# A PSUM bank for the weight conversion's intermediate, taken from the attention's products with v

## The chip, the cores and the metric

The kernel runs on one core of one Trainium2 chip. The metric is the device time of one launch in microseconds (us), lower is better. The core has TensorE (PE in the profile) for matmuls, VectorE (DVE), ScalarE (ACT) and GpSimd (POOL) for elementwise work, and SyncE (SP), which here only issues transfers. The engines run their own instruction rows in order and wait for one another through semaphores. Tiles live in SBUF or in PSUM; PSUM has eight banks of 2 KB a partition, and one bank holds 512 float32 values a partition.

## The reference

Sixteen attention heads (2 batches of 8, 768 tokens, head size 64) attend only inside hash buckets, and two gated MLPs follow (1536 tokens, model size 512, hidden size 2048):

```python
q_bits = (np.einsum('bhsd,dk->bhsk', q, proj) > 0); k_bits = (np.einsum('bhsd,dk->bhsk', k, proj) > 0)
mask = q_bucket[:, :, :, None] == k_bucket[:, :, None, :]        # the six bits read as a number
scores = np.where(mask, scale * np.matmul(q, k.transpose(0, 1, 3, 2)), -1e9)
x = softmax(scores) @ v                                           # heads side by side: 1536 x 512
h = x @ w_in;  g = h * (1.0 / (1.0 + np.exp(-1.702 * h)));  x = g @ w_out
h = x @ w_in2; g = h * (1.0 / (1.0 + np.exp(-h)));          out = g @ w_out2
```

The four weight matrices arrive as 64-bit floats. The kernel turns them into 32-bit ones itself.

## The kernel before, in words

**Stages.** The first batch's attention runs first, alone (to about 145 us of the span). Then the second batch's attention runs with the first MLP of the first batch's tokens laid between its steps (to about 415 us): this is the stretch that the change touches, and it is called the mixed stretch below. After it come the rest of that MLP, the first MLP of the second batch's tokens, and the second MLP.

**Attention.** A step is one head and one block of 128 query tokens. `scores` (L414, L415) puts a step's 128x768 scores into a `pss` tile of two banks; DVE's `top` (L422) takes them out to `p` and finds the extreme of each row, ACT takes the exponential (L427) and a half-precision copy `hl` (L438), POOL the remainder of that copy (L442), and a transposing transfer brings both as `pt` (L448). `av` (L460 to L462) multiplies `pt` with the head's v, three matmuls for each of six blocks of keys, into `pav`. All the steps of a head (half of them for the last two heads of a batch) go to one `pav` bank and make a group. `norm` (L472 to L476) divides the group's products by their sums on DVE. After every second head `x_turn` (L488) transposes the result through a `psx` bank and `x_split` (ACT L494, DVE L495) takes it out of there. In the mixed stretch there is one `pss` tile, so a step's scores wait until the DVE has taken the last step's.

**MLP.** `gemm1` (L624) makes twelve matmuls into a `psh` bank for a block of 384 tokens and 128 hidden units. ACT (L629) and DVE (L630) gate it, ACT and POOL split it (L634, L635). `gemm2` (L658) multiplies with the second weight matrix, and DVE adds the result to `part` (L667). Every product is made of three matmuls of a high and a low part.

**Weights.** A chunk is 128x512 weights. `Weights.step` fetches a chunk to `raw` (L139) and converts it: ACT takes the absolute value of the upper words (L170), four DVE operations of 128x512 elements follow, clamp (L171), shift (L172), and two that merge in words of `raw` (L173, L175), each rewriting the SBUF tile `f`; then ACT writes the high part (L177) and POOL the low part (L178). `f` has two buffers. There are 64 chunks, 28 of which the change touches; of the others four come before the point of the program at which the mixed stretch begins, and 32 belong to the second MLP.

**Who sets the order.** The program lists its work step by step; a scheduler then sorts each engine's instructions, with priorities by kind of task (the table SOONER, left as it is). `RATE` sets how many MLP pieces go with one attention step, and a chunk is converted with each piece while there is room for it.

**PSUM.** In the mixed stretch the banks are: two for `m` (`pstr`, the transposes of q and k, and `psbit`), two for `av` (`pav` and `psx` in turn), two for `pss`, two for `psh` and `pso`.

Of the kernel before, what the change touches and what calls it, by code (L numbers as in the profile page):

```python
# [9 lines left out]
F32 = mybir.dt.float32  # L10
F32R = mybir.dt.float32r
F16 = mybir.dt.float16
I32 = mybir.dt.int32
I64 = mybir.dt.int64
AF = mybir.ActivationFunctionType
ALU = mybir.AluOpType
AX = mybir.AxisListType
PSUM = bass.MemoryType.PSUM
# [3 lines left out]
def tile_lsh_attention_two_mlps(  # L22
# [13 lines left out]
    V, A, G, T, SP = nc.vector, nc.scalar, nc.gpsimd, nc.tensor, nc.sync  # L36
# [5 lines left out]
    P = 128  # L42
# [5 lines left out]
    NDC = DM // P  # L48
# [9 lines left out]
    TINY = 2.0 ** -15  # L58
    HUGE = 122880.0 - 2.0 ** -7
# [47 lines left out]
    class Weights:  # L107
# [41 lines left out]
        def step(self):  # L149
            n = self.done  # L150
            depth = 3 if late[0] is not None else 1
            while self.issued <= min(n + depth, len(self.chunks) - 1):
                self.fetch()
            i, kind = self.chunks[n]
            pool = self.pool_of(i)[0]
            hi = pool.tile([P, NDC, P], F32R, tag=f"w{kind}h", name=f"w{kind}h")
            lo = pool.tile([P, NDC, P], F32R, tag=f"w{kind}l", name=f"w{kind}l")
            block = self.order[i]
            self.t[i, kind] = hi, lo
            self.done += 1  # L160
            if self.again(n):
                for t, d in zip((hi, lo), self.kept.pop((block, kind))):
                    SP.dma_start(out=t.bitcast(F32), in_=d)
                return
            raw = self.raw.pop(n)
            word = raw.bitcast(I32).rearrange("p c (e w) -> p c e w", w=2)
            f = (late[0] or wpool).tile([P, NDC, P], F32, tag="f", name="f", bufs=2 if late[0] else FB)
            fi = f.bitcast(I32)
            top, bot = word[:, :, :, 1], word[:, :, :, 0]
            A.activation(f, top.bitcast(F32), AF.Abs)  # L170
            V.tensor_scalar(f, f, TINY, HUGE, op0=ALU.max, op1=ALU.min)  # L171
            V.tensor_scalar(fi, fi, 3, 0x3FFFFFFF, op0=ALU.logical_shift_left, op1=ALU.bitwise_and)  # L172
            V.scalar_tensor_tensor(out=fi, in0=top, scalar=-0x40000000, in1=fi,  # L173
                                   op0=ALU.bitwise_and, op1=ALU.bitwise_or)
            V.scalar_tensor_tensor(out=fi, in0=bot, scalar=29, in1=fi,  # L175
                                   op0=ALU.logical_shift_right, op1=ALU.bitwise_or)
            A.copy(hi, f)  # L177
            G.tensor_tensor(out=lo, in0=f, in1=hi.bitcast(F32), op=ALU.subtract)  # L178
            if self.last[block] > i:
                self.kept[block, kind] = []  # L180
                for t, part in ((hi, "h"), (lo, "l")):
                    d = spill.tile([P, NDC, P], F32, name=f"sp{kind}{part}{block[1]}")
                    SP.dma_start(out=d, in_=t.bitcast(F32))
                    self.kept[block, kind].append(d)
# [64 lines left out]
    def attention(sp, s1, ps_m, ps_v, ahead_of, setup):  # L249
        nat, st = {}, {}  # L250
# [4 lines left out]
        for n in range(0, HEADS, 2):  # L255
            parts = 2 if n % H == H - 2 else 1
            for half in range(parts):
                for h in (n, n + 1):
                    w = NC // parts
                    g = tuple(range(len(steps), len(steps) + w))  # L260
# [4 lines left out]
        count = {"nv": 0}  # L265
# [94 lines left out]

        def rows_at_once(half):
            for nm, i, w in (("k", 0, thr), ("q", 2, thrq)):
                ps = ps_v.tile([P, 512], F32, tag="av", name="psbit")
                o, cols = ps[0:R, 0:HS], slice(i * R, (i + 1) * R)
                T.matmul(o, lhsT=pa[i][:, cols], rhs=st[nm, 0][:, half], start=True, stop=False)
                T.matmul(o, lhsT=pb[i][:, cols], rhs=st[nm, 0][:, half], start=False, stop=True)
                dst = (BQ if nm == "q" else BK)[0]
                V.tensor_scalar(dst[0:R, half * HS:(half + 1) * HS], o, w[0:R, 0:1], w[0:R, 1:2],
                                op0=ALU.is_ge, op1=ALU.mult)
# [81 lines left out]
        def av(j):  # L451
            (n, c), g = steps[j], group[j]
            vs, s = st["v", n // 2]
            pt = st.pop(("pt", j))
            if j == g[0]:
                st["av", g] = ps_v.tile([P, 512], F32, tag="av", name="pav")
            o = st["av", g][:, c * (D + 1):(c + 1) * (D + 1)]
            for i in range(NC):
                hv, lv = vs[:, n % 2, i, 0:D + 1], vs[:, n % 2, i, D + 1:]
                T.matmul(o, lhsT=pt[:, i], rhs=hv, start=(i == 0), stop=False)  # L460
                T.matmul(o[:, 0:D], lhsT=pt[:, i], rhs=lv, start=False, stop=False)
                T.matmul(o, lhsT=pt[:, NC + i], rhs=hv, start=False, stop=(i == NC - 1))  # L462
# [20 lines left out]
                    x_split(pr, half)  # L483

        def x_turn(pr, half):
            ps = ps_v.tile([P, 512], F32, tag="av", name="psx")
            for d in range(HC):
                T.transpose(ps[:, d * P:(d + 1) * P], st["x", pr][:, half * HC + d].rearrange("p j d -> p (j d)"), ident)  # L488
            st["px", pr, half] = ps[:, 0:HS]
# [6 lines left out]


        asked = set()

        def ahead(pr, s):  # L500
            a, b = 2 * pr, 2 * pr + 1
# [34 lines left out]
        for n in (0, 1):  # L536
# [15 lines left out]
            for half in range(2):  # L552
                if n == 0:
                    rows_at_once(half)
                else:
                    bits(0, half, (1, 3))
                    signs(0, half)
# [17 lines left out]
        for lead, first, last in ((2, 0, N // 2), (1, N // 2, N)):  # L575
# [5 lines left out]
            for i in range(first - lead, last + LAG + 1):  # L581
# [4 lines left out]
                m = i - LAG  # L586
# [3 lines left out]
                m = i - 2 * (2 - lead)  # L590
# [98 lines left out]
    again = [NF - 1 - RING - i for i in range(NF - RING)]  # L689
    order = [(0, f) for f in range(NF)] + [(0, f) for f in again] + [(1, f) for f in range(NF)]  # L690
    late = [None]

    def pool_of(i):
        if i < NF:
            return wpool, i - RING if i >= RING else None
        slot = (i - NF) % (RING + RING2)
        before = i - RING - RING2
        if slot < RING2:
            return late[0], before if before >= NF else None
        return wpool, before if before >= NF else NF - RING + slot - RING2  # L700
# [6 lines left out]
    def background():  # L707
        if W.can_step():
            with sooner("weights"):
                W.step()  # L710

    with ExitStack() as es:
        ps_m = es.enter_context(tc.tile_pool(name="ps_m", bufs=2, space=PSUM))
        ps_v = es.enter_context(tc.tile_pool(name="ps_v", bufs=2, space=PSUM))
        sp = es.enter_context(tc.tile_pool(name="att", bufs=2))
        s1 = es.enter_context(tc.tile_pool(name="att1", bufs=1))
        ps_s = ExitStack()
        am = ps_s.enter_context(tc.tile_pool(name="att2", bufs=1))
        ahead_of = {"lead": 2, "more": {t: (am, MORE[t]) for t in MORE if MORE[t]}}
        ahead_of["pool"] = ps_s.enter_context(tc.tile_pool(name="ps_s", bufs=2, space=PSUM))  # L720
        gen, credit = None, 0.0
        for i in attention(sp, s1, ps_m, ps_v, ahead_of, lambda: attention_setup(sp, s1, am, ps_m)):
            if i == -2:
                for _ in range(EARLY):
                    W.fetch()
            if gen is None and i >= WSTART and i % WEVERY == 0 and W.done < 4:
                W.step()
            if gen is None and i == SWITCH - 1:
                ps_s.close()
                stage[0] = 1  # L730
                ahead_of["lead"] = 1
                ahead_of["more"] = {}
                mb = es.enter_context(tc.tile_pool(name="mlpb", bufs=2))
                ahead_of["pool"] = es.enter_context(tc.tile_pool(name="ps_s1", bufs=1, space=PSUM))
                ps_h = es.enter_context(tc.tile_pool(name="ps_h", bufs=2, space=PSUM))
                gen = mlp(0, [0, 1], [[f, f + 1] for f in range(0, NF, 2)], W, mb, ps_h, True, first1)
            if gen is not None:
                credit += RATE[i >= 3 * HEADS // 4 * NC]
                while credit >= 1.0:
                    credit -= 1.0  # L740
                    next(gen, None)
                    background()
        for _ in gen:
            background()
    stage[0] = 2
    late[0] = ctx.enter_context(tc.tile_pool(name="w2", bufs=RING2))
    mp = ctx.enter_context(tc.tile_pool(name="mlp", bufs=2))
    ps_h = ctx.enter_context(tc.tile_pool(name="ps_h", bufs=8, space=PSUM))
# [35 lines left out]
```

## Time and profile before

| what | value |
|---|---|
| time, median of 3 runs | 829.68 us (829.2 to 832.83) |
| the profiled execution: its time, its span | 829.76 us, 827.9 us |
| granted TensorE clock, mean | 0.965 |
| PE busy: whole span; 0 to 145, 145 to 415, 415 to 828 us | 748.4; 108.87, 235.72, 403.78 us |
| DVE busy in the same stretches | 539.1; 117.04, 229.18, 192.89 us |
| ACT busy | 421.9; 99.25, 174.63, 147.97 us |
| POOL busy | 443.2; 94.13, 189.60, 159.47 us |

The profiled execution lies 0.08 us above the median, and its span leaves 1.9 us around it. The stretches are read with one row of a table that gives each engine's busy time in each window. "Busy" covers an instruction from its start to its end, so time in which it is held up after its start counts as busy too.

### The profile page before, as it was taken

The page shows a single profiled execution, that of the slowest core. Times are in us where ns is not written, and L with a number is a line of the kernel's source. Part 1 is how long each engine was busy: PE and PEld are TensorE (multiplying, and loading weights), DVE is VectorE, ACT ScalarE, POOL GpSimd, SP SyncE. Part 2 cuts the span into 40 slices and gives each one's busy share as a digit, 9 for nine tenths or more (in the row PEclk, how much of TensorE's full clock was granted, in tenths as well). Part 3 has the DMA queues.
Part 4 walks back from the last instruction along what each step waited for, and adds up shares of the span by engine and source line. Part 5 has one row for each costly group of instructions (what it writes and reads, how often), then busy time and mean ns, then how long its engine had stood idle before and what let it go on. Part 6 is the DMA issues. An engine that isn't in the chain of part 4 may idle for free.

```text
span 827.9 us, 14002 instructions
## 1 busy us (share of the span) xinstructions
PE 748.4 (90%) x5384; PEld 687.0 (83%) x5384; DVE 539.1 (65%) x932; ACT 421.9 (51%) x721; POOL 443.2 (54%) x345
## 2 busy tenths in 40 slices
PE   6786787688888989898999999979999999999998
PEld 5675666678787878787999999978999889988996
DVE  8886788889799988888524243899733843422222
ACT  5776567585766757566544232444545423321220
POOL 5675576777766767566733242648534533421120
PEclk9898998799999999999999999999999999999999
DMA  5999999999989878874688431233310300000112
GB/s 155 198 198 187 185 215 199 239 251 252 252 211 243 221 210 204 204 168 79 115 285 287 141 114 40 84 120 101 103 51 28 126 1 1 0 1 1 39 39 76
DMA packets 196270, 116.40 MB, mean 141 GB/s; under 512 B 153318, under 2 KB 175846, under 8 KB 196204
## 3 DMA queue, kind: packets, MB, share of 16 engines
q1 hardware_dynamic: 196044, 115.52, 55.3%
q8 instruction: 42, 0.69, 0.3%
q14 instruction: 24, 0.20, 0.1%
q10 hardware_dynamic: 160, 0.00, 0.0%
HBM read 56.63 MB, written 16.78 MB: 89 GB/s over the span
## 4 chain that ended last, share of the span: by engine, by line
PE 59%; DVE 20%; DMA 8%; issue 6%; ACT 5%; POOL 2%; SPq 0%; DVEq 0%; ACTq 0%; POOLq 0%
PE pso L658 26%; PE psh L624 25%; DMA pt<-hl 5%; DVE f L173 3%; DVE p L422 3%; DVE f L171 3%; DVE f L175 2%; DVE f L172 2%; DMA raw<-in_moe_w_in_dram 2%; PE pss L414 2%; DVE part L667 1%; ACT p L427 1%; PE psbit L342 1%; PE pss L415 1%; PE pav L460 1%
## 5 line engine op out<-in xcount | busy, mean ns | idle before, releaser
L635 POOL TENSOR_TENSOR gl<-g,gh 128x384 fp32r<-128x384 f32 x128 | 138.3, 1082 | 195.1 <-ACT gh L634 182.3
L442 POOL TENSOR_TENSOR hl<-p,hl 128x768 f16<-128x768 f32 x96 | 168.0, 1757 | 83.3 <-ACT hl L438 38.3
L624 PE MATMUL psh<-XH,wih 128*128 128x384 f32 x512 | 174.7, 341 | 2.9 <-DVE part L667 2.9
L624 PE MATMUL psh<-XL,wih 128*128 128x384 f32 x512 | 173.6, 339 | 2.2 <-DVE XL L495 2.2
L624 PE MATMUL psh<-XH,wil 128*128 128x384 f32 x512 | 173.7, 339 | 0.0
L633 DVE TENSOR_TENSOR g<-g,psh 128x384 f32<-128x384 f32 x96 | 52.8, 551 | 117.3 <-ACT g L632 117.3
L667 DVE SCALAR_TENSOR_TENSOR part<-pso,part 128x384 f32<-128x384 f32 (+1 forms) x124 | 72.5, 590 | 83.6 <-PE pso L658 83.4
L427 ACT ACTIVATE p<-p,lo 128x768 f32<-128x768 f32 x96 | 89.6, 937 | 69.8 <-DVE p L422 69.6
L634 ACT CAST gh<-g 128x384 fp32r<-128x384 f32 x128 | 65.5, 512 | 84.0 <-DVE g L633 70.2
L658 PE MATMUL pso<-gh,woh 128*128 128x384 f32 x256 | 89.0, 354 | 15.2 <-DVE g L630 5.5
L624 PEld LDWEIGHTS psh<-XH,wih 128*128 128x128 f32 x512 | 97.6, 191 | 4.4 <-DVE part L667 2.6
L624 PEld LDWEIGHTS psh<-XL,wih 128*128 128x128 f32 x512 | 97.5, 190 | 3.1 <-DVE XL L495 2.5
L422 DVE TENSOR_SCALAR_CACHE_REDUCE p<-pss 128x768 f32<-128x768 f32 x96 | 90.4, 946 | 12.1 <-PE pss L415 9.9
L624 PEld LDWEIGHTS psh<-XH,wil 128*128 128x128 f32 x512 | 97.6, 191 | 0.2 <-POOL wil L178 0.2
L632 ACT ACTIVATE g<-psh 128x384 f32<-128x384 f32 x96 | 46.8, 489 | 97.0 <-PE psh L624 96.0
L414 PE MATMUL pss<-ak,aq 128*128 128x384 f32 x192 | 76.4, 399 | 18.1 <-DVE p L422 17.8
L460 PE MATMUL pav<-VS,pt 128*128 128x65 f16 x576 | 65.1, 200 | 25.8 <-DMA pt<-hl 24.5
L658 PE MATMUL pso<-gh,wol 128*128 128x384 f32 x256 | 86.5, 338 | 0.0
L658 PE MATMUL pso<-gl,woh 128*128 128x384 f32 x256 | 86.5, 338 | 0.0
L460 PEld LDWEIGHTS <-pt 128*128 128x128 f16 x576 | 54.7, 100 | 33.7 <-DMA pt<-hl 28.5
L658 PE MATMUL pso<-woh,gh 128*128 128x512 f32 x192 | 74.8, 390 | 0.3 <-ACT gh L634 0.3
L658 PE MATMUL pso<-wol,gh 128*128 128x512 f32 x192 | 75.0, 391 | 0.0
(114 smaller groups left out, 1616.9 us busy)
## 6 DMA issues: line engine op xcount, KB each, us to landing
raw<-in_moe_w_in_dram SPq DMA_DIRECT2D x32, 512.0 KB
raw<-in_moe_w_out_dram SPq DMA_DIRECT2D x32, 512.0 KB
spih<-wih SPq DMA_DIRECT2D x13, 256.0 KB
spil<-wil SPq DMA_DIRECT2D x13, 256.0 KB
spoh<-woh SPq DMA_DIRECT2D x13, 256.0 KB
spol<-wol SPq DMA_DIRECT2D x13, 256.0 KB
wih<-spih SPq DMA_DIRECT2D x13, 256.0 KB
wil<-spil SPq DMA_DIRECT2D x13, 256.0 KB
```

The source lines that it names most:

```text
L414: T.matmul(o, lhsT=lq, rhs=ak[:, half, :], start=True, stop=False)
L422: V.tensor_scalar(p, st.pop(("S", j)), LOW, None, op0=ALU.min, op1=ALU.min, accum_out=lo)
L427: A.activation(p, p, AF.Exp, bias=lo, scale=-1.0)
L442: G.tensor_tensor(out=hl[:, 1], in0=st.pop(("p", j))[0], in1=hl[:, 0], op=ALU.subtract)
L460: T.matmul(o, lhsT=pt[:, i], rhs=hv, start=(i == 0), stop=False)
L624: T.matmul(h, lhsT=a[:, c], rhs=x[t][:, c], start=(n == 0), stop=(n == 3 * NDC - 1))
L632: A.activation(g, h, AF.Sigmoid, scale=beta)
L633: V.tensor_tensor(out=g, in0=g, in1=h, op=ALU.mult)
L634: A.copy(gh[:, f], g)
L635: G.tensor_tensor(out=gl[:, f], in0=g, in1=gh[:, f].bitcast(F32), op=ALU.subtract)
L658: T.matmul(y, lhsT=a, rhs=x, start=(n == 0), stop=(n == 3 * nf - 1))
L667: V.scalar_tensor_tensor(out=acc, in0=y, scalar=scale, in1=acc, op0=ALU.mult, op1=ALU.add)
```

## The change

The tile `f` is split in two roles. A new tile `u` takes the absolute value and the three in-place operations; the fourth one reads `u` and writes `f`, which ACT and POOL then read from SBUF as before. In the mixed stretch `u` is a PSUM tile of one bank with one buffer; everywhere else `u` is `f` itself, and the instructions are what they were.

The bank comes from `av`. Its pool of two buffers becomes two pools of one, used in turn by `v_bank`. At the start of the mixed stretch the second is closed: `pav` then has one bank, and `x_turn` takes its `psx` from the two `m` banks.

```diff
+            u = work[0].tile([P, NDC, P], F32, tag="u", name="u") if work[0] is not None else f
+            ui = u.bitcast(I32)
-            A.activation(f, top.bitcast(F32), AF.Abs)
-            V.tensor_scalar(f, f, TINY, HUGE, op0=ALU.max, op1=ALU.min)
-            V.tensor_scalar(fi, fi, 3, 0x3FFFFFFF, op0=ALU.logical_shift_left, op1=ALU.bitwise_and)
-            V.scalar_tensor_tensor(out=fi, in0=top, scalar=-0x40000000, in1=fi,
+            A.activation(u, top.bitcast(F32), AF.Abs)
+            V.tensor_scalar(u, u, TINY, HUGE, op0=ALU.max, op1=ALU.min)
+            V.tensor_scalar(ui, ui, 3, 0x3FFFFFFF, op0=ALU.logical_shift_left, op1=ALU.bitwise_and)
+            V.scalar_tensor_tensor(out=ui, in0=top, scalar=-0x40000000, in1=ui,
                                    op0=ALU.bitwise_and, op1=ALU.bitwise_or)
-            V.scalar_tensor_tensor(out=fi, in0=bot, scalar=29, in1=fi,
+            V.scalar_tensor_tensor(out=fi, in0=bot, scalar=29, in1=ui,
                                    op0=ALU.logical_shift_right, op1=ALU.bitwise_or)
...
-                ps = ps_v.tile([P, 512], F32, tag="av", name="psbit")
+                ps = v_bank("psbit")
...
-                st["av", g] = ps_v.tile([P, 512], F32, tag="av", name="pav")
+                st["av", g] = v_bank("pav")
...
-            ps = ps_v.tile([P, 512], F32, tag="av", name="psx")
+            ps = v_bank("psx") if len(ps_v) > 1 else ps_m.tile([P, 512], F32, tag="m", name="psx")
...
+        def v_bank(name):
+            j = count["av"] = (count.get("av", -1) + 1) % len(ps_v)
+            return ps_v[j].tile([P, 512], F32, tag="av", name=name)
...
-        ps_v = es.enter_context(tc.tile_pool(name="ps_v", bufs=2, space=PSUM))
+        ps_v = [es.enter_context(tc.tile_pool(name="ps_v", bufs=1, space=PSUM))]
...
+        ps_v.append(ps_s.enter_context(tc.tile_pool(name="ps_x", bufs=1, space=PSUM)))
...
                 ps_s.close()
+                ps_v.pop()
...
+                work[0] = es.enter_context(tc.tile_pool(name="ps_w", bufs=1, space=PSUM))
...
     stage[0] = 2
+    work[0] = None
```

The scheduler sorts the rows anew. Row texts carry each program's own line numbers: L170 to L173, L175 and L177 of before are L173 to L176, L178 and L180 of the changed kernel, L422 is L425, L427 is L430, L438 is L441, and L629, L630 and L634 are L637, L638 and L642.

First, DVE's row early in the mixed stretch, before: conversions (`f`), scores taken out (`p`) and gates (`g`).

```order
L175 SCALAR_TENSOR_TENSOR f<-raw,f 128x512
L171 TENSOR_SCALAR f<-f 128x512
L172 TENSOR_SCALAR f<-f 128x512
L630 SCALAR_TENSOR_TENSOR g<-g,psh 128x384
L173 SCALAR_TENSOR_TENSOR f<-raw,f 128x512
L422 TENSOR_SCALAR p,lo<-pss 128x768
L175 SCALAR_TENSOR_TENSOR f<-raw,f 128x512
L422 TENSOR_SCALAR p,lo<-pss 128x768
```

The same place in the changed kernel's DVE row:

```order
L174 TENSOR_SCALAR u<-u 128x512
L175 TENSOR_SCALAR u<-u 128x512
L176 SCALAR_TENSOR_TENSOR u<-raw,u 128x512
L638 SCALAR_TENSOR_TENSOR g<-g,psh 128x384
L178 SCALAR_TENSOR_TENSOR f<-raw,u 128x512
L425 TENSOR_SCALAR p,lo<-pss 128x768
L174 TENSOR_SCALAR u<-u 128x512
L175 TENSOR_SCALAR u<-u 128x512
```

The four operations of a chunk stand in the same sequence between the same neighbours; there are as many of them as before.

Second, ACT's row in the same part of the program, before: the absolute value of a chunk (`f<-raw`) and the high part of a chunk (`wih<-f`, `woh<-f`) among the attention's and the gate's rows.

```order
L177 CAST wih<-f 128x512
L629 ACTIVATE g<-psh 128x384
L170 ACTIVATE f<-raw 128x512
L427 ACTIVATE p<-p,lo 128x768
L634 CAST gh<-g 128x384
L438 CAST hl<-p 128x768
L629 ACTIVATE g<-psh 128x384
L170 ACTIVATE f<-raw 128x512
```

And in the changed kernel:

```order
L180 CAST woh<-f 128x512
L173 ACTIVATE u<-raw 128x512
L642 CAST gh<-g 128x384
L430 ACTIVATE p<-p,lo 128x768
L637 ACTIVATE g<-psh 128x384
L441 CAST hl<-p 128x768
L642 CAST gh<-g 128x384
L180 CAST wih<-f 128x512
L173 ACTIVATE u<-raw 128x512
```

Before, two absolute values could stand one behind the other, with the high part of neither between them. Now each stands right behind the high part of the chunk before it, since there is one `u`.

On PE the MLP's matmuls stand later against the attention's. When three quarters of the products with v are issued, 216 matmuls of `gemm1` and 174 of `gemm2` stand ahead of them before, 192 and 156 now. At the last product with v it is 384 and 366 before, 384 and 360 now.

More of the change, by code (lines that the diff above doesn't have):

```diff
@@ L691, in tile_lsh_attention_two_mlps @@
     late = [None]
+    work = [None]
     def pool_of(i):
```

## The prediction

> **What bounds the kernel now.** First I read busy time by stretch, to see where an engine is full.
>
> ```profile
> core 0: us, PE busy (x) PEld busy (x) DVE busy (x) ACT busy (x) POOL busy (x), PEclk, DMA share, GB/s
> 145.00:190.00 45.00, 35.88 (x353) 32.49 (x354) 39.00 (x67) 31.61 (x51) 35.61 (x24) 0.85 1.12 242
> 190.00:235.00 45.00, 38.14 (x319) 34.30 (x317) 39.85 (x60) 28.17 (x49) 31.78 (x23) 0.96 0.98 255
> ...
> 145.00:415.00 270.00, 235.72 (x2084) 215.53 (x2085) 229.18 (x383) 174.63 (x285) 189.60 (x135) 0.96 0.86 203
> ...
> 415.00:828.00 413.00, 403.78 (x2133) 379.26 (x2132) 192.89 (x299) 147.97 (x289) 159.47 (x140) 1.00 0.24 82
> ```
>
> After 415 us PE is busy 403.78 of 413 us: that stretch is PE's own work, and nothing in this change makes it shorter. In the mixed stretch (145 to 415 us) no engine is full: PE 235.72, DVE 229.18, POOL 189.60 of 270 us. PE idles 270 - 235.72 = 34.3 us there, and that is where a gain can come from. The next view says for whom PE waited in that window.
>
> ```profile
> PE pss L414 <- DVE p L422: 10.7, 10, 2.9
> PE pav L460 <- DMA pt<-hl: 6.6, 3, 3.7
> PE pso L658 <- DVE g L630: 5.5, 4, 2.6
> PE pso L658 <- DVE part L667: 4.8, 7, 1.8
> PE psh L624 <- DVE part L667: 2.2, 2, 1.8
> PE psh L624 <- DVE XL L495: 2.2, 1, 2.2
> PE psx L488 <- DVE xn L476: 1.3, 1, 1.3
> ```
>
> The six rows that name the DVE add up to 10.7 + 5.5 + 4.8 + 2.2 + 2.2 + 1.3 = 26.7 us. None of them waits for a conversion: they wait for attention and MLP rows that stand behind conversions in DVE's row. What a conversion costs there is in the DVE's groups of the same window (busy us, then mean ns of one); the last row is a group of the stretch after 415 us to hold them against.
>
> ```profile
> L422 DVE TENSOR_SCALAR_CACHE_REDUCE p<-pss 128x768 f32<-128x768 f32 x50 | 47.3, 947 | 5.4 <-PE pss L415 4.5 <-POOL wol L178 0.9
> L173 DVE SCALAR_TENSOR_TENSOR f<-raw,f 128x512 int32<-128x512 int32 x31 | 37.6, 1212 | 0.3
> L175 DVE SCALAR_TENSOR_TENSOR f<-raw,f 128x512 int32<-128x512 int32 x31 | 34.3, 1107 | 0.3
> L172 DVE TENSOR_SCALAR f<-f 128x512 int32<-128x512 int32 x31 | 28.1, 905 | 0.5
> L171 DVE TENSOR_SCALAR f<-f 128x512 f32<-128x512 f32 x30 | 24.4, 813 | 11.8 <-ACT f L170 11.7
> ...
> L495 DVE TENSOR_TENSOR XL<-psx,XH 128x384 fp32r<-128x384 f32 x9 | 4.8, 550 | 2.0 <-ACT XH L494 2.0
> ...
> L667 DVE SCALAR_TENSOR_TENSOR part<-pso,part 128x512 f32<-128x512 f32 x36 | 24.9, 690 | 58.3 <-PE pso L658 58.3
> ```
>
> A chunk costs 1212 + 1107 + 905 + 813 = 4037 ns of DVE. The spread of each row shows that this is not its work alone (the columns are minimum, median and maximum in ns).
>
> ```profile
> L172 DVE TENSOR_SCALAR f<-f x31: 409/429/1882, 145.4 to 378.3; 128x512 int32<-128x512 int32 x31
> L173 DVE SCALAR_TENSOR_TENSOR f<-raw,f x31: 675/1282/2026, 147.3 to 378.7; 128x512 int32<-128x512 int32 x31
> L175 DVE SCALAR_TENSOR_TENSOR f<-raw,f x31: 645/1075/2031, 149.8 to 382.0; 128x512 int32<-128x512 int32 x31
> ...
> L171 DVE TENSOR_SCALAR f<-f x30: 412/703/1916, 154.4 to 377.3; 128x512 f32<-128x512 f32 x30
> ```
>
> The minima add up to 412 + 409 + 675 + 645 = 2141 ns, so a chunk is held up for 4037 - 2141 = 1896 ns on average. By whom, the timeline shows at one place (start, length):
>
> ```profile
> 258.30 2.10 POOL L442 TENSOR_TENSOR hl<-p,hl 128x768 f16<-128x768 f32 x1
> 258.92 2.02 DVE L175 SCALAR_TENSOR_TENSOR f<-raw,f 128x512 int32<-128x512 int32 x1
> ```
>
> POOL's instruction ends at 260.40, and L175 ends 0.54 us later, as if it had begun its work only then. An instruction that also has a PSUM operand does not show this:
>
> ```profile
> L630 DVE SCALAR_TENSOR_TENSOR g<-g,psh x32: 536/545/555, 170.5 to 407.8; 128x384 f32<-128x384 f32 x32
> ```
>
> The gate reads one SBUF and one PSUM tile. Between 536 and 555 ns, in 32 runs beside a POOL that is busy 70% of the time (189.60 of 270), it was never held up. The Trainium skill (SBUF — State Buffer, Who interferes with whom) says that a DVE instruction with two SBUF inputs, or one in a mode that uses two SBUF ports, and a GpSimd instruction lock each other out, and that one with at most one SBUF input outside those modes does not. The trace agrees: L175 took 2.02 us, L630 never over 0.56 us.
>
> **The change part by part.**
>
> *DVE's conversions.* Three of the four now work on PSUM in and out, and the fourth reads PSUM. I price each at the 690 ns of L667 in its 128x512 form, which reads PSUM and SBUF and is of the same size: 4 x 690 = 2760 ns a chunk. That is 619 ns more than the minima (the clamp and the shift lose 280 ns each) and 4037 - 2760 = 1277 ns less than the mean in this stretch. For 28 chunks that is 28 x 1.277 = 35.8 us less DVE time. The Trainium skill (VectorE: DVE Perf Modes, Why PSUM operands drop a tier) speaks against the change here: a PSUM operand takes float32 to one element a cycle, while an SBUF-to-SBUF clamp runs at two. L171's minimum of 412 against L667's 690 ns agrees. By that page alone, with nobody in the way, the 28 chunks would cost 28 x 0.619 = 17.3 us more DVE time, not less.
>
> How much of 35.8 us lies on the path? The chain of waits that ended last, in the mixed stretch, answers it by line:
>
> ```profile
> by line: issue 13.4%; PE pso L658 9.1%; DVE p L422 7.7%; DVE f L173 7.7%; PE psh L624 7.3%; DVE f L171 6.5%; DVE f L172 5.3%; DVE f L175 4.9%; DMA raw<-in_moe_w_in_dram 3.7%; DVE part L667 3.3%; DMA pt<-hl 2.7%; DVE g L630 2.5%; PE pss L414
> ...
> 389.90 4.16 PE psh L624 x24
> ```
>
> The four conversion rows hold 7.7 + 6.5 + 5.3 + 4.9 = 24.4% of 270 us = 65.9 us, of the 37.6 + 34.3 + 28.1 + 24.4 = 124.4 us that they are busy: 53%. So 0.53 x 35.8 = 19.0 us come off that chain. The ends are nothing, if a parallel path is just as long, and the 26.7 us that PE waits for the DVE at all. I take 19.0, since it lies between them and is read from the path itself.
>
> *POOL.* It is no longer held up by the conversions either. Nothing is booked: it idles 270 - 189.60 = 80 us, so its own time is not the bound.
>
> *ACT.* Its absolute value is written to PSUM in place of SBUF, as often as before. No row shows ACT writing PSUM; its two SBUF forms of that size differ by 674 - 618 = 56 ns (rows below), so I book no difference, for ends of 28 x 0.06 = 1.6 us either way, which ACT's 270 - 174.63 = 95 us of idle time cover. With one `u` each absolute value now waits for the last DVE operation of the chunk before. It stands directly behind that chunk's high part, which waits for the same operation, so ACT's row is held up no longer than before; what stands behind it are the exponentials and the copies of the next attention step. A chunk's turn is then 0.62 + 0.67 us on ACT (high part, absolute value), 2.76 us on the DVE, and in between about one L422 and one gate (0.95 + 0.55 us): 5.55 us. The 28 chunks have 270 / 28 = 9.6 us each, so this chain is covered.
>
> ```profile
> L170 ACT ACTIVATE f<-raw x30: 647/674/691, 152.8 to 373.8; 128x512 f32<-128x512 f32 x30
> L177 ACT CAST wih<-f x16: 602/618/633, 144.7 to 378.9; 128x512 fp32r<-128x512 f32 x16
> ```
>
> *Weights come later.* In the order that the scheduler gives PE, 24 + 18 = 42 MLP matmuls have moved behind the three-quarter mark of the mixed stretch's products with v. At 4.16 / 24 = 0.173 us each (the row above) that is 7.3 us of PE work moved from where PE idles to where it idles less. Its price lies between 0 and 7.3 us; I take 2, because the attention in front of the mark is shorter by the same work. Six matmuls of `gemm2` move behind the last product with v: 6 x 0.173 = 1.0 us.
>
> *One bank for `pav`.* The first product of a group now waits until `norm` has read the last group. The trace of before shows what there is to lose; at the tightest hand-over:
>
> ```profile
> 337.28 0.20 PE L460 MATMUL pav<-VS,pt 128*128 128x65 f16 x1 [1.77 <-DMA pt<-hl]
> ...
> 337.40 0.54 DVE L476 TENSOR_TENSOR xn<-pav,ri 128x384 f32<-128x384 f32 x1
> ```
>
> The next group's product began at 337.28, and `norm` was through at 337.94: one bank would have cost 0.66 us here, with the MLP's matmuls queued behind on PE. At the widest one the product came 394.60 - 386.96 = 7.6 us after `norm`; seven lie between.
>
> ```profile
> 386.60 0.36 DVE L476 TENSOR_TENSOR xn<-pav,ri 128x192 f32<-128x192 f32 x1
> ...
> 394.60 0.20 PE L460 MATMUL pav<-VS,pt 128*128 128x65 f16 x1
> ```
>
> I book 1 us in all, and keep 0 and 6 (0.66 at each of nine) as ends.
>
> *`psx` in the `m` banks.* A transposed half now holds one of the two banks that the transposes of q and k and the hash bits use, until ACT and DVE have read it (L495 takes 550 ns), in three pairs of heads; in the last pair there are no such transposes left. Three pairs by two halves by 0.55 us is 3.3 us at most, 0 at least; I book 1.
>
> Sum: 19.0 - 2 - 1 - 1 - 1 = 14.0 us. Against the profiled execution's 829.76 us (0.08 above the median, so the median needs no correction) that is 815.8, rounded to 816.
>
> **The rivals.**
>
> *Transfers take over.* The DMA share is 1.12 and 0.98 in the first 90 us of the mixed stretch, so a DVE that is quicker may there only wait for `pt` and `raw`. For it: 6.6 us of PE waits are for `pt`, and `raw` has 3.7% of the chain. Against it: the DVE is busy 39 of 45 us there all the same. Then only 180 of 270 us gain: 19.0 x 2/3 - 5 = 7.7 us, 822.
>
> *The order eats the gain.* The PE work that moved (7.3 us), the hand-overs (6) and the `m` banks (3.3) cost their upper ends: 19.0 - 7.3 - 1 - 6 - 3.3 = 1.4 us, 828. The change then does what it says on the DVE, and the end stays.
>
> *The other side: a conversion on PSUM is held up by POOL all the same.* If the lock hangs on the instruction and not on its SBUF inputs, each chunk keeps its 1896 ns and loses the 619 ns of the faster forms: 0.53 x 17.3 = 9.2 us, and the 5 us of charges come on top: 829.8 + 14.2 = 844. It decides from a mean of 1.01 us for one operation on `u` (4037 / 4): above it the kernel is slower. L630 speaks against it.
>
> *The change doesn't do what it says*, as the bank or `u` could come too late or not at all: the changed order shows 28 chunks on `u`, so I give it nothing.
>
> **How the numbers follow.** My forecast, 816, has a chance of 0.61; transfers 0.16; the eaten gain 0.13; the held-up conversion 0.10. Half a per cent of 829.68, 4.1 us, is about what a measurement of this kernel can tell from no change: faster is below 825.5, slower above 833.8. Faster is 0.61 + 0.16 = 0.77, same 0.13, slower 0.10. The low end is all 26.7 us of PE's waits gone: 803. The high end takes in the eaten gain, 828, and leaves the slower case out; about 0.15 lies outside.
>
> **What would show it.** Right: the operations on `u` at 650 to 720 ns with hardly a spread; DVE busy in the mixed stretch down by some 36 us; `pss` <- L422 and the other waits for the DVE down by half or more; PE's last product with v near 400 us in place of 415. Wrong: operations on `u` with maxima of 2 us (held up all the same); a new wait of `pav` L460 for `xn` L476 of over 5 us, or of `pstr` or `psbit` for `XL` L495 (the bank was needed); waits for `pt` and `raw` that grow by what the DVE's lose (transfers). A span that ends as before with a shorter DVE would mean that the chain through the conversions was not the one that bounds the mixed stretch.

## The result, and the profile after

The changed kernel takes 809.92 us (median of 4 runs, 808.29 to 811.03) against 829.84 us for the kernel before on the same chips. The ratio is 0.9751, with a 95% interval of 0.9723 to 0.978. Its profiled execution took 809.91 us, with a span of 807.9 us in place of 827.9.

In the table of busy time by stretch, the mixed stretch now ends at about 394 us in place of 415. The columns are those of the table of before.

```profile
core 0: us, PE busy (x) PEld busy (x) DVE busy (x) ACT busy (x) POOL busy (x), PEclk, DMA share, GB/s
...
145.00:395.00 250.00, 226.73 (x2104) 210.31 (x2104) 197.40 (x385) 174.71 (x284) 176.44 (x134) 0.98 0.95 220
395.00:808.00 413.00, 403.70 (x2133) 379.20 (x2131) 191.19 (x297) 148.67 (x290) 159.96 (x140) 1.00 0.24 82
```

The last 413 us are what they were (403.70 us of PE against 403.78). All of the 20 us went out of the mixed stretch. PE's idle time there fell from 34.3 to 250 - 226.73 = 23.3 us, which is 11 us. The other 9 us are PE's own busy time, 235.72 before and 226.73 now, for nearly the same matmuls: six of `gemm2` have moved behind the end, and 17 that used to start before 145 us now start after it (1151 in place of 1168 stand ahead of that mark).

The operations on `u` in the view by tile (minimum, median, maximum in ns):

```profile
L174 DVE TENSOR_SCALAR u<-u x28: 678/694/700, 181.2 to 364.4; 128x512 f32<-128x512 f32 x28
L175 DVE TENSOR_SCALAR u<-u x28: 679/692/700, 182.4 to 365.6; 128x512 int32<-128x512 int32 x28
L176 DVE SCALAR_TENSOR_TENSOR u<-raw,u x28: 678/692/697, 183.9 to 366.8; 128x512 int32<-128x512 int32 x28
L178 DVE SCALAR_TENSOR_TENSOR f<-raw,u x28: 643/681/687, 184.6 to 369.0; 128x512 int32<-128x512 int32 x28
```

No operation took over 700 ns, where maxima of 1882 to 2031 stood before. DVE's busy time fell from 229.18 to 197.40 us, which is 31.8 us where some 36 were forecast. What PE waits for in the mixed stretch:

```profile
PE pav L463 <- DMA pt<-hl: 15.3, 12, 3.0
PE pss L417 <- DVE p L425: 2.3, 3, 1.5
PE psh L632 <- DVE XL L498: 1.8, 1, 1.8
PE pso L666 <- DVE part L675: 1.5, 1, 1.5
...
PE psh L632 <- DVE part L675: 0.3, 1, 0.3
```

The waits for the DVE fell from 26.7 to 2.3 + 1.8 + 1.5 + 0.3 = 5.9 us. Those for the transposed `pt` rose from 6.6 to 15.3 us. No wait of `pav` for `xn` and none of `pstr` or `psbit` for `XL` is among PE's waits. The chain of waits by line in this window says who took the place of the conversions:

```profile
by line: DMA pt<-hl 20.1%; PE pso L666 16.9%; PE psh L632 13.5%; DMA raw<-in_moe_w_in_dram 4.4%; issue 4.0%; PE pss L417 3.4%; PE psbit L345 3.3%; PE pss L418 3.0%; DMA raw<-in_moe_w_out_dram 2.9%; PE pav L463 2.9%; DVE p L425 2.5%; PE pav 
```

The four conversion rows, 24.4% before, are no longer among the first; the transfers of `pt` have gone from 2.7 to 20.1%.

### The profile page after: what moved, and what is told of

It reads as the page before. It is cut to its first block, busy times and chain, and to the rows that moved or that the text cites. A ratio compares the mean times of both kernels' runs of the same rounds, so it can differ in the third digit from the quotient of the medians.

```text
span 807.9 us, 14034 instructions
## 1 busy us (share of the span) xinstructions
PE 740.4 (92%) x5384; PEld 682.6 (84%) x5384; DVE 507.3 (63%) x932; ACT 422.4 (52%) x721; POOL 430.4 (53%) x345
## 4 chain that ended last, share of the span: by engine, by line
PE 66%; DMA 13%; DVE 10%; issue 4%; ACT 3%; POOL 2%; SPq 0%; ACTq 0%; DVEq 0%; POOLq 0%
PE pso L666 29%; PE psh L632 28%; DMA pt<-hl 9%; PE pss L417 2%; PE psbit L345 2%; POOL hl L445 2%; DMA raw<-in_moe_w_in_dram 2%; DVE p L425 2%; PE pss L418 2%; DVE f L176 1%; ACT p L430 1%; PE pav L463 1%; PE pav L464 1%; PE pav L465 1%; DVE f L175 1%
## 5 line engine op out<-in xcount | busy, mean ns | idle before, releaser
L643 POOL TENSOR_TENSOR gl<-g,gh 128x384 fp32r<-128x384 f32 x128 | 136.0, 1064 | 195.7 <-ACT gh L642 183.6
L445 POOL TENSOR_TENSOR hl<-p,hl 128x768 f16<-128x768 f32 x96 | 162.6, 1700 | 71.9 <-ACT hl L441 37.4
L430 ACT ACTIVATE p<-p,lo 128x768 f32<-128x768 f32 x96 | 89.7, 936 | 52.7 <-DVE p L425 52.2
L642 ACT CAST gh<-g 128x384 fp32r<-128x384 f32 x128 | 65.5, 513 | 78.7 <-DVE g L641 69.1
L425 DVE TENSOR_SCALAR_CACHE_REDUCE p<-pss 128x768 f32<-128x768 f32 x96 | 90.8, 948 | 15.3 <-PE pss L418 13.3
L666 PE MATMUL pso<-gh,woh 128*128 128x384 f32 x256 | 87.3, 347 | 6.5 <-ACT gh L642 4.3
```

The costliest lines, as they stand in the source:

```text
L425: V.tensor_scalar(p, st.pop(("S", j)), LOW, None, op0=ALU.min, op1=ALU.min, accum_out=lo)
L430: A.activation(p, p, AF.Exp, bias=lo, scale=-1.0)
L445: G.tensor_tensor(out=hl[:, 1], in0=st.pop(("p", j))[0], in1=hl[:, 0], op=ALU.subtract)
L642: A.copy(gh[:, f], g)
L643: G.tensor_tensor(out=gl[:, f], in0=g, in1=gh[:, f].bitcast(F32), op=ALU.subtract)
L666: T.matmul(y, lhsT=a, rhs=x, start=(n == 0), stop=(n == 3 * nf - 1))
```

## The experiments

Theory: POOL held up the conversions that work within SBUF, and a PSUM operand frees them. First rival: the gain comes from the new order of rows and banks. Second rival: the lost bank costs several microseconds, which the conversions overpay. The scheduler sorts the rows of each of these kernels anew, so a run differs from its parent by its edit and by the order that came with it; where the order matters, the matmuls that stand ahead of the last product with v are counted from the trace. Each median stands beside one of the kernel before on the same chip (830.1 to 830.7 us).

**The bank change alone.**

```diff
-            u = work[0].tile([P, NDC, P], F32, tag="u", name="u") if work[0] is not None else f
+            u = f
```

> All of the change but the conversion's place: pav has one bank, psx lies in the m banks, a PSUM bank lies idle, and the conversion works in the SBUF tile f as before. If the gain comes from the conversions no longer being held up by POOL and the bank is free of charge: 828 to 832 us, a conversion's operations at 0.8 to 1.2 us mean as before. If the lost bank costs what was booked for it (hand-overs, m banks: 2 us, up to 9): 832 to 839. If the gain came from the new order of the rows or of the banks: under 818.

Measured: 826.74 us, ratio 0.9958 (0.994 to 0.9975). The loss of a `pav` bank costs nothing; the run is even 3 us faster than before. PE's waits:

```profile
PE pav L463 <- DMA pt<-hl: 10.5, 9, 3.0
PE pss L417 <- DVE p L425: 6.8, 5, 2.7
PE pso L666 <- DVE g L638: 6.6, 4, 2.6
PE psh L632 <- DVE part L675: 4.1, 4, 1.2
```

`pav` waits for `pt`, not for `norm`, and the DVE is still waited for. The conversions take 750 to 1191 ns on average, as held up as before. The second rival falls. Of the first rival, the banks have at most 3 us; this run's order is nearer to that of before (366 matmuls of `gemm2` ahead of the last product with v, as in the kernel before, against 360 in the change), so it says nothing on the change's order.

**The same program with `u` in SBUF.**

```diff
-                work[0] = es.enter_context(tc.tile_pool(name="ps_w", bufs=1, space=PSUM))
+                work[0] = es.enter_context(tc.tile_pool(name="wu", bufs=1))
```

> The changed kernel with u as a single SBUF tile of its own in place of the PSUM bank, nothing else. Same instructions, same single buffer, same banks. If PSUM is what frees the DVE: 827 to 835 us, the operations on u with means of 0.8 to 1.2 us and maxima near 2 us. If splitting u from f, or having one u and so a different order, made the gain: under 818 us whatever the means.

Measured: 829.87 us, ratio 0.9987 (0.9966 to 1.0008): no difference from before. The groups in its mixed stretch (busy us, mean ns):

```profile
L176 DVE SCALAR_TENSOR_TENSOR u<-raw,u 128x512 int32<-128x512 int32 x28 | 36.0, 1287 | 0.6
L178 DVE SCALAR_TENSOR_TENSOR f<-raw,u 128x512 int32<-128x512 int32 x28 | 28.9, 1031 | 3.3 <-POOL wol L181 2.7
L175 DVE TENSOR_SCALAR u<-u 128x512 int32<-128x512 int32 x28 | 25.8, 923 | 0.4
L174 DVE TENSOR_SCALAR u<-u 128x512 f32<-128x512 f32 x28 | 23.8, 850 | 6.7 <-ACT u L173 6.7
```

A chunk costs 1287 + 1031 + 923 + 850 = 4091 ns, about as much as before. The program has the change's tiles, single buffer and banks, so none of these makes the gain. But the scheduler made another order for it: 378 matmuls of `gemm2` stand ahead of the last product with v, against 360 in the change. The difference of 829.87 - 809.92 = 20 us is therefore that of the memory together with the order that came with it.

**POOL writes and reads nothing**, in the kernel before, for the remainder of `p` in the second batch (L442). The kernel leaves out the low half of the probabilities there.

```diff
-            G.tensor_tensor(out=hl[:, 1], in0=st.pop(("p", j))[0], in1=hl[:, 0], op=ALU.subtract)
+            if stage[0] == 1:
+                st.pop(("p", j))
+                G.memset(hl[:, 1], 0.0)
...
```

> The kernel before, with POOL's remainder of p in the second batch replaced by a memset to zero of the same tile (the low half of the probabilities is left out of the second batch's products). POOL then reads no SBUF there, and is busy for a shorter time. If POOL is what holds the DVE up: the two merges fall from 1212 and 1107 to under 950 ns mean, and the time below 826 us. If the DVE was slow for another reason (the memory of raw, the transfers): the means stay within 5% of before.

Measured: 820.08 us (one run). The conversions, in SBUF as before:

```profile
L173 DVE SCALAR_TENSOR_TENSOR f<-raw,f 128x512 int32<-128x512 int32 x31 | 25.0, 807 | 0.5
L175 DVE SCALAR_TENSOR_TENSOR f<-raw,f 128x512 int32<-128x512 int32 x32 | 22.6, 706 | 0.4
L172 DVE TENSOR_SCALAR f<-f 128x512 int32<-128x512 int32 x31 | 19.9, 641 | 0.5
L171 DVE TENSOR_SCALAR f<-f 128x512 f32<-128x512 f32 x30 | 15.7, 523 | 17.9 <-ACT f L170 17.9
```

All four fell, 4037 to 807 + 706 + 641 + 523 = 2677 ns, without anything being changed on the DVE. So it was POOL's instructions that held them up. POOL is also shorter at work here, but the trace of this run separates reading from being busy. A merge and a shift, each beside memsets (start, length; x2 is two of them):

```profile
227.23 1.45 POOL L444 MEMSET hl<- 128x768 f16 x2 [0.18 <-DMA pt<-hl]
228.19 0.67 DVE L173 SCALAR_TENSOR_TENSOR f<-raw,f 128x512 int32<-128x512 int32 x1
349.16 1.68 POOL L444 MEMSET hl<- 128x768 f16 x2 [3.42 <-DMA pt<-hl]
350.28 0.84 DVE L172 TENSOR_SCALAR f<-f 128x512 int32<-128x512 int32 x1
```

All 16 merges that began during a memset took 673 to 693 ns, their quiet time; the six that began with over 0.1 us of a reading POOL instruction ahead took 1272 to 1767. A merge, then, is held up by POOL's reading. The shift above ended 0.28 us behind the memset, and so did the one clamp that began during one: for these two, a POOL instruction that only writes is enough.

The trace of the kernel before says the same for each operation, and more sharply than the means. In its mixed stretch 69 of the 123 conversion operations began with over 0.1 us of a POOL instruction ahead. Every one of them ended a fixed time behind that instruction: 278 to 292 ns for clamp and shift, 544 to 551 ns for the merges. The other 54 took 409 to 694 ns. In the changed kernel 75 of the 112 operations on `u` began beside a running POOL instruction, and all 112 took 643 to 700 ns.

**The merges and the shift's output on PSUM, the absolute value and the clamp in `f`.**

```diff
-            A.activation(u, top.bitcast(F32), AF.Abs)
-            V.tensor_scalar(u, u, TINY, HUGE, op0=ALU.max, op1=ALU.min)
-            V.tensor_scalar(ui, ui, 3, 0x3FFFFFFF, op0=ALU.logical_shift_left, op1=ALU.bitwise_and)
+            A.activation(f, top.bitcast(F32), AF.Abs)
+            V.tensor_scalar(f, f, TINY, HUGE, op0=ALU.max, op1=ALU.min)
+            V.tensor_scalar(ui, fi, 3, 0x3FFFFFFF, op0=ALU.logical_shift_left, op1=ALU.bitwise_and)
```

> The absolute value and the clamp stay in f (SBUF), the shift reads f and writes u (PSUM), the two merges as in the change. If only a second SBUF stream lets POOL hold an instruction up: shift and merges at 680 to 700 ns with no spread, the clamp still at 0.7 to 0.9 us mean with maxima over 1.3 us; per chunk 2.8 to 3.0 us, 809 to 814 us. If any SBUF input of a one-input operation is held up: the shift at 0.9 us mean or more with maxima near 1.9 us, 813 to 818 us.

Measured: 818.97 us, ratio 0.9863 (0.9836 to 0.9889). The durations are as the theory has them, in the mixed stretch (the merges took 689 and 677 ns on average):

```profile
L174 DVE TENSOR_SCALAR f<-f x30: 412/428/1397, 153.3 to 356.5; 128x512 f32<-128x512 f32 x30
L175 DVE TENSOR_SCALAR u<-f x28: 673/687/696, 176.4 to 360.3; 128x512 int32<-128x512 int32 x28
```

Only the clamp, SBUF to SBUF, is still held up at times. The time is not as expected: 9 us above the change, though DVE spends no more on the conversions. That clamp, the longer use of `f` or the new order can cost this: 384 matmuls of `gemm2` stand ahead of the last product with v, 24 more than in the change.

**All four operations with a PSUM side, only the absolute value in `f`.** The clamp then reads `f` and writes `u`.

```diff
-            A.activation(u, top.bitcast(F32), AF.Abs)
-            V.tensor_scalar(u, u, TINY, HUGE, op0=ALU.max, op1=ALU.min)
+            A.activation(f, top.bitcast(F32), AF.Abs)
+            V.tensor_scalar(u, f, TINY, HUGE, op0=ALU.max, op1=ALU.min)
```

> The changed kernel, with the absolute value written to f in SBUF and the clamp reading f and writing u. No operation of the conversion uses a second SBUF stream, as in the change, but f is taken from the absolute value on, as in the kernel before and in the run with merges only (819 us). If what that run lost was the clamp still locked against POOL: 808 to 813 us here. If it was f being held longer, so that conversions start later: 816 to 821 us, all operations at 680 to 700 ns.

Measured: 820.84 us, ratio 0.9881 (0.9863 to 0.99). Its first two operations:

```profile
L174 DVE TENSOR_SCALAR u<-f x28: 672/692/695, 176.9 to 365.9; 128x512 f32<-128x512 f32 x28
L175 DVE TENSOR_SCALAR u<-u x28: 676/692/699, 177.6 to 367.5; 128x512 int32<-128x512 int32 x28
```

Nothing is held up, and 11 us of the gain are gone all the same. So it isn't the clamp. The order is again one with 384 matmuls of `gemm2` ahead of the last product with v. ACT waits longer in front of the absolute value:

```profile
ACT f L173 <- DMA raw<-in_moe_w_in_dram: 15.8, 7, 5.2
ACT f L173 <- DMA raw<-in_moe_w_out_dram: 9.6, 5, 3.2
```

That is 25.4 us, against these two rows of the changed kernel:

```profile
ACT u L173 <- DMA raw<-in_moe_w_in_dram: 6.8, 2, 3.8
ACT u L173 <- DMA raw<-in_moe_w_out_dram: 2.9, 2, 2.2
```

**The same with a third buffer for `f`.**

```diff
-            f = (late[0] or wpool).tile([P, NDC, P], F32, tag="f", name="f", bufs=2 if late[0] else FB)
+            if work[0] is not None and n % 3 == 2:
+                f = work[1].tile([P, NDC, P], F32, tag="f", name="f")
+            else:
+                f = (late[0] or wpool).tile([P, NDC, P], F32, tag="f", name="f", bufs=2 if late[0] else FB)
```

> The run with the absolute value in f (820.8 us), with a third buffer for f in the mixed stretch. Same operations, same durations (680 to 700 ns). If that run lost its 11 us because f is taken from the absolute value until POOL's low part is done, and two buffers are too few for that: 807 to 814 us, ACT's waits for raw in front of the absolute value down from 25 us to under 15. If it lost them to something else in the new order of the rows: 817 to 824 us.

Measured: 816.16 us, ratio 0.9823 (0.9796 to 0.9851), between the two ranges expected. Less than half of the 11 us came back, and ACT waits for `raw` as long as without the third buffer:

```profile
ACT f L176 <- DMA raw<-in_moe_w_in_dram: 13.7, 9, 2.8
ACT f L176 <- DMA raw<-in_moe_w_out_dram: 12.4, 10, 2.4
```

The 5 us are real, since the interval of this run and that of the two-buffer one (0.9863 to 0.99) don't meet. Whether they are the price of holding `f` isn't shown: in the new order 360 matmuls of `gemm2` stand ahead of the last product with v, as in the change, so 24 x 0.173 = 4.2 us of PE work left the stretch at the same time. Where the other 6 us are stays open. Its mixed stretch (145 to 400 us) idles no more on PE than the change's, 255 - 232.93 = 22.1 us, but PE is busy for 232.93 us in place of 226.73, at a granted clock of 0.96 in place of 0.98:

```profile
145.00:400.00 255.00, 232.93 (x2081) 213.53 (x2082) 193.02 (x382) 173.03 (x282) 174.95 (x134) 0.96 0.91 214
```

**The clamp done twice**, in the changed kernel's mixed stretch.

```diff
             V.tensor_scalar(u, u, TINY, HUGE, op0=ALU.max, op1=ALU.min)
+            if work[0] is not None:
+                V.tensor_scalar(u, u, TINY, HUGE, op0=ALU.max, op1=ALU.min)
```

> The changed kernel with the clamp on u done twice in the mixed stretch (a second clamp changes nothing): 28 x 0.69 = 19 us more DVE time, no other engine touched. If the DVE is off the path now and transfers and PE bound the stretch: 811 to 815 us. If DVE time is still worth 0.53 us per us, as the sum of the prediction took it: 818 to 823 us.

Measured: 834.82 us, ratio 1.006 (1.0027 to 1.0093): 24.9 us above the change for 19 us of DVE, more than either expected. The matmuls of `gemm1` behind the last product with v, in this run and then in the changed kernel:

```profile
388.20:835.00 446.80, 220.31 (x1224) 215.15 (x1224) 0.99 0.23 78
```

```profile
393.80:808.00 414.20, 206.36 (x1152) 202.25 (x1152) 1.00 0.24 82
```

The attention ends 6 us earlier, at 388 us, but 1224 - 1152 = 72 matmuls of `gemm1`, and 72 of `gemm2` in the same view, have moved behind it, and that last part takes 447 us in place of 414. So the cost is one of order: the scheduler lets the conversions, and the MLP with them, come later. ACT never waits for the last operation on `u` in this trace, so it isn't a wait at the single buffer on the chip. Whether the scheduler moved them for the longer chain or for the DVE's time this run doesn't tell.

**The absolute value taken twice**, so that ACT pays and not the DVE.

```diff
             A.activation(u, top.bitcast(F32), AF.Abs)
+            if work[0] is not None:
+                A.activation(u, u, AF.Abs)
```

> The changed kernel with the absolute value taken twice on ACT, in place on u: each chunk's chain is longer by about 0.63 us, as with the doubled clamp, but ACT pays and not the DVE (ACT idles 75 us in the mixed stretch). If the chain of a chunk bounds: MLP matmuls move behind the last product with v again, 820 to 836 us. If DVE time does: 809 to 814 us.

Measured: 836.50 us, ratio 1.0067 (1.0049 to 1.0085). `gemm1` behind the last product with v:

```profile
390.40:835.00 444.60, 217.31 (x1200) 212.50 (x1200) 0.99 0.23 77
```

Again 1200 - 1152 = 48 of `gemm1` (and 72 of `gemm2`) are late, without any DVE time added. What the two runs have in common is the longer chain through the single `u`, and in both its price shows as a later MLP in the scheduler's order.

**A reduction that nobody waits for**, with each chunk of the mixed stretch, in the changed kernel and then in the one before.

```diff
             A.copy(hi, f)
+            if work[0] is not None:
+                idle = wpool.tile([P, 1], F32, tag="idle", name="idle", bufs=1)
+                V.tensor_reduce(out=idle, in_=XH[0].rearrange("p c t -> p (c t)")[:, 0:512].bitcast(F32), axis=AX.X, op=ALU.max)
```

> The changed kernel, and for each of the 28 chunks a DVE reduction over 512 elements of a finished tile that nobody waits for: about 28 x 0.68 = 19 us more DVE time, as in the doubled clamp, but outside the conversion's chain. The doubled clamp cost 25 us, with 144 MLP matmuls pushed behind the last product with v. If it is the chain of a chunk that costs (one u, four operations one behind the other): 809 to 815 us here. If it is DVE time as such: 820 to 836.

> The same 28 or so reductions in the kernel before. Its DVE is busy 229 of 270 us in the mixed stretch. If DVE time is what bounds it, each us costs about 0.5 us or more (the chain's share): 838 to 850 us, and clearly more than the same reductions cost in the changed kernel. If the conversions cost through their length and not through DVE time: 829 to 835.

Measured: 822.34 us in the changed kernel (ratio 0.9882, 0.9849 to 0.9915), 843.91 us in the one before (1.0161, 1.0126 to 1.0197). The view by tile shows that the runs missed their place:

```profile
L183 DVE TENSOR_REDUCE idle<-XH x28: 649/672/681, 106.8 to 176.0; 128x1 f32<-128x512 f32 x28
```

```profile
L180 DVE TENSOR_REDUCE idle<-XH x28: 648/672/682, 104.3 to 175.5; 128x1 f32<-128x512 f32 x28
```

Since the reductions depend on little, the scheduler put all 28 between 104 and 176 us, 16 and 17 of them ahead of the mixed stretch. What they price is DVE time at that place: (822.34 - 809.92) / 18.8 = 0.66 us per us in the changed kernel and (843.91 - 830.66) / 18.9 = 0.70 in the one before (the 28 take 18.8 and 18.9 us). Both prices are rough, since in both runs 18 more matmuls of `gemm2` than in the parent stand ahead of the last product with v. The expectation of the chain theory (809 to 815) is missed too: the chain is not the only thing that costs. DVE time was not clearly dearer in the kernel before, as had been expected.

**Products with v four steps behind the scores.**

```diff
-    LAG = 3
+    LAG = 4
```

> The changed kernel with the products with v issued four steps behind the scores in place of three. In the changed kernel PE waits 15 us for the transposed pt in the mixed stretch. If that wait is the new bound of the stretch: PE's wait for pt falls below 8 us and the time to 800 to 807 us. If the transfers are only as late as the steps that feed them: 807 to 813 us, pt still waited for.

Measured: 816.79 us, ratio 0.9823 (0.978 to 0.9867), slower than the change. PE's wait, and the two stretches:

```profile
PE pav L463 <- DMA pt<-hl: 16.4, 11, 3.1
```

```profile
145.00:390.00 245.00, 219.10 (x2022) 202.65 (x2021) 186.78 (x372) 169.26 (x274) 166.54 (x127) 0.96 0.97 225
390.00:816.00 426.00, 416.38 (x2204) 391.51 (x2203) 196.66 (x308) 153.59 (x299) 167.11 (x148) 1.00 0.24 80
```

The wait for `pt` stays; the attention ends 4 us sooner with less of the MLP beside it, which then comes behind it. That the row that is waited for longest now is the next bound is not borne out by this remedy.

**`u` on PSUM in the second MLP too.**

```diff
-    work[0] = None
+    work[0] = ctx.enter_context(tc.tile_pool(name="ps_w2", bufs=1, space=PSUM))
...
-    ps_h = ctx.enter_context(tc.tile_pool(name="ps_h", bufs=8, space=PSUM))
+    ps_h = ctx.enter_context(tc.tile_pool(name="ps_h", bufs=7, space=PSUM))
```

> The changed kernel, and in the second MLP's stretch u has a PSUM bank too (the products there have seven banks in place of eight). The conversions there fall from about 3.25 to 2.76 us a chunk, 32 chunks, 16 us of DVE time. If a gain is to be had only where PE idles for the DVE (it idles 9 of 413 us after 395 us): 806 to 811 us. If DVE time is worth the same everywhere (0.53 us per us): 800 to 803 us. If seven banks are too few: over 812 us.

Measured: 800.27 us, ratio 0.9629 (0.96 to 0.9659). This is faster than both kernels; its interval lies below the change's. Its two stretches:

```profile
391.00:799.00 408.00, 403.22 (x2146) 379.07 (x2142) 181.35 (x300) 149.08 (x291) 151.06 (x142) 1.00 0.24 83
145.00:391.00 246.00, 227.43 (x2076) 210.34 (x2077) 196.53 (x381) 174.59 (x284) 175.27 (x133) 0.97 0.95 223
```

PE's idle time in the last stretch fell from 413 - 403.70 = 9.3 to 4.8 us; the changed kernel's longest wait there, 4.5 us of `pso` for ACT's `gh`, is gone. That stretch, from the last product with v, takes 407.7 us in place of 414.1. The other 2.6 us of the 9 between the spans lie ahead of it, where the rows of the two programs are the same on every engine (up to 415 us): that much two executions of one order can differ. The time fits the expectation that DVE time is worth something everywhere (800 to 803).

## Why the prediction was right, point by point

**The bound.** Right: the mixed stretch lost 20 us and the last one nothing. The ceiling was drawn too low, though. The prediction took PE's idle time as all that could be gained; 9 of 20 us came out of PE's busy time. Going from a granted clock of 0.96 to 0.98 would account for 235.72 x (1 - 0.96 / 0.98) = 4.8 us of them, an estimate from clocks rounded to 0.01; whether the change raised the clock no run separates, and the rest isn't attributed.

**The conversions.** Right in mechanism and size: 694 + 692 + 692 + 681 = 2759 ns a chunk by the medians, against 2760 forecast, and nothing held up. The run with `u` in SBUF shows the same instructions held up again. That POOL does the holding is shown by the memset run and by the fixed time between POOL's end and that of each held operation.

**The path's share.** 53% of 35.8 us, 19.0, came out near the 20 us measured. The nearness is in part luck: the run with the absolute value in `f` has the same DVE time and gains 10 us only. The three kernels with held-up conversions (before, the bank alone, `u` in SBUF) took 826.7 to 830.7 us. Four with the conversions freed and no work added (the change, the absolute value in `f`, the third `f`, and the merges only, where the clamp is still held up) took 809.9 to 820.8, each in an order of its own. So freeing them pays in every order on record: 6 us between the closest two, 10 to 20 against the kernel before. Which end it is depends on the order and on how long `f` is held; the runs don't separate the two, and the sum had no term for either. DVE time has no one price either: a rough 0.66 to 0.70 us per us around the start of the stretch.

**The charges.** This is the mis-sized term. Of the 5 us booked, the hand-over of `pav` (1) and the `m` banks (1) measured nothing: the bank change alone ran 3 us faster than before. The tail was 413.0 before and 414.1 us now, as the 1 us booked for the six matmuls of `gemm2`. For the late weights 2 us were booked; no run separates them. Without the first two charges the sum is 16 us, still short of 20.

**The chain of a chunk, called covered.** No wait at `u` of more than 2.2 us stood in the change, so it was covered on the chip, but nearer the edge than 5.55 of 9.6 us says: the conversions run from 181 to 369 us, 28 in 188, 6.7 us each. In the scheduler's order 0.58 to 0.69 us more per chunk pushed 120 to 144 matmuls out of the stretch and cost 25 to 27 us.

**The rivals.** Transfers did come forward: PE's waits for `pt` went from 6.6 to 15.3 us. They gave back 8.7 of the 20.8 us that the waits for the DVE lost, not the third of the gain that the rival took. The gain was not eaten by the order, and no operation on `u` was held up.

## What to carry to other kernels

Where a group of DVE instructions has a mean near twice its minimum beside a busy POOL, look at what the row reads, and whether the long ones end a fixed time behind POOL's instruction: here the same operation took 690 ns with one operand in PSUM and 0.8 to 1.3 us with all in SBUF, and its quiet time, 410 ns for two of the four, was the wrong number to compare. A bank given up costs what waits for it: read the gap between its last reader and its next writer before booking a price. A buffer count of one is a chain; its slack is seen in the spacing of the chunks, and lengthening it by one operation is a cheap test. Where a scheduler sorts the rows, compare the orders too before a difference is put down to the edit: here kernels with equal conversions lay 11 us apart.

## What the runs showed of the hardware

POOL was held up by the conversions as well, and gained too. In the mixed stretch its remainder of `p` before:

```profile
L442 POOL TENSOR_TENSOR hl<-p,hl 128x768 f16<-128x768 f32 x52 | 92.4, 1781 | 48.9 <-ACT hl L438 23.3 <-issue 15.4 <-PE pso L658 5.7
```

and after:

```profile
L445 POOL TENSOR_TENSOR hl<-p,hl 128x768 f16<-128x768 f32 x52 | 87.3, 1680 | 37.2 <-ACT hl L441 22.9 <-issue 6.4 <-POOL gl L643 2.0
```

One takes 1680 in place of 1781 ns, and the idle time in front of it that nothing explains fell from 15.4 to 6.4 us. Of the 52 before, 22 began while a conversion was running, and took 1864 ns in the median; the other 30 took 1657. Of those after, 12 began beside an operation on `u`, and took 1642 to 1671 ns. ACT's absolute value of 128x512 took 634 ns from SBUF into PSUM (median of 28), 674 within SBUF, and 582 within PSUM in the run that takes it twice. A shift from SBUF to PSUM took 687 ns, never over 696, beside the same POOL that held the same shift within SBUF up to 1882.
